# E over two queues, F as fp16 behind the first k loads, and three places of a Linformer-attention and maxout kernel reordered

## The chip, the core and the metric

The kernel runs on one core of a Trainium2 chip. The time is the device time of one execution in microseconds, as the median of several runs. A profile of one execution, with every instruction and DMA packet, goes with it.

## The reference

Attention with keys and values projected along the sequence (Linformer), and behind it a maxout block. All inputs and the output are float32.

```python
k_proj = np.einsum('ks,bhsd->bhkd', E, k)          # E, F: 64 x 1024
v_proj = np.einsum('ks,bhsd->bhkd', F, v)          # q, k, v: 8 batches, 8 heads, 1024, 64
scores = scale * np.matmul(q, k_proj.transpose(0, 1, 3, 2))
attn = np.exp(scores - np.max(scores, axis=-1, keepdims=True))
attn = attn / (np.sum(attn, axis=-1, keepdims=True) + 1e-09)
attn_out = np.matmul(attn, v_proj)
x = attn_out.transpose(0, 2, 1, 3).reshape(B * S, H * D)     # 8192 x 512
h1, h2 = x @ w1, x @ w2                                      # 512 x 1024 each
return np.maximum(h1, h2) @ w_out                            # 1024 x 512
```

## The kernel before

**Algebra.** max(h1, h2) is h2 + relu(h1 - h2). The kernel forms wd = w1 - w2 (`step_wd`, L437) and m = w2 w_out once, and then for each piece of x it computes gt = relu(x wd) (the "up" product) and out = gt w_out + x m (the "down" product). From the second batch on, each of these products of 2x2 blocks is done with seven block products instead of eight, p1 to p7 in the order p1, p2, p6, p5, p7, p3, p4. They need sums of blocks, S(0) to S(3), made by VectorE (`sum_s`, L595), and they share PSUM banks: a bank X takes p1, and p6, p7 and p4 are accumulated onto it in turn; Z takes p5 and then p3; Y takes p2. Each time a bank is to be read before the next product is accumulated, ScalarE copies it to SBUF (`keep`, L607 and L609): s1 after p1, u1 after p6, u2 after p7, s5 after p5. VectorE's `add` (L650 for up, L750 for down) joins two of them into a block.

**Units.** Each of the eight batches has two units, 0 to 15. Unit n's down product is interleaved on TensorE with unit n+1's up product and with the attention of the batches ahead. The interleaving is an order written out by hand: `slots` is a list of keys and functions. ("P", n, p, i) is piece i of down product p of unit n, ("U", n, h, i) the i-th up step of half h, ("G", n, h) a group of attention. `at_slot` hangs further work behind a key. The loop at L906 lays out, for each half h, x pieces, the group, y pieces, and then seven up steps with a piece between each two.

**A group of attention.** `step_group` (L352) issues scores for one group into PSUM banks 2 and 3 (L277) and sums and values for the one before (`step_da`, L380; L289). ScalarE then takes the exponentials of the scores (L370) and the logarithm of the sums (L389). `step_later` runs what `step_da` left for later: at ("U", n, h, 0) the reciprocal by an exponential of minus the logarithm (`invert`, L392), at ("U", n, h, 2) VectorE's multiplication (`finish`, L396).

**Up product p3** of unit n+1 (L673) adds block (0,1), and then, from u2 and s5, block (1,1), each followed by a relu (L653) in the last two units. p4 goes from its bank straight through ScalarE's relu (L690). The sums S(0) and S(1) of the next down product are issued behind them.

**The last unit** has no up product beside its down product (`alone`). There p5 comes before p6 (L812), p5 goes to bank 2, p3 is stored in one piece through ScalarE's queue, and p4 is made in three parts (L792 matmuls, L798 adds) with stores on SyncE's and ScalarE's queues. Its banks are X = 1, Y = 0.

**The start.** SyncE's queue loads E and F as float32 into 64 partitions (L89, L90). GpSimd's queue loads k, q and v of batch 0 in pieces of two heads, cast to fp16 on the way (L101): two k, two q, the identity matrix (made by GpSimd itself, masks.py), two k, two q, four v, then the weights w2 and w1 in pieces (L124, L133). GpSimd's queue holds about eight loads: each further issue waits for the landing of the one eight before. TensorE warms up on a tile of ones (`warm`, L147), transposes E and F in fp32 through the identity (L161), eight transposes each, and VectorE copies the first and ScalarE the second result to one tile `eft` (L168). `step_kv` (L189) multiplies it with k and v, `step_kpt` (L222) and `step_qt` (L248) transpose the projected k and q, `step_sc` makes the scores.

Of the kernel before, what the change touches and what calls it, by code (L numbers as in the profile page):

```python
# [8 lines left out]
FP32 = mybir.dt.float32  # L9
# [7 lines left out]
def kernel(  # L17
# [12 lines left out]
    nc = tc.nc  # L30
# [34 lines left out]
    def att_banks(dtype=FP32):  # L65
# [4 lines left out]
    ctx.enter_context(tc.manual_schedule())  # L70


    nc.scalar.add_instruction(
        mybir.InstLoadActFuncSet(
            name=nc.get_next_instruction_name(),
# [3 lines left out]
            outs=[],  # L79
        )  # L80
    )

    def big(n, dtype=FP16):
        return const.tile([128, 16384 // mybir.dt.size(dtype) // 2], dtype, tag=f"big{n}", name=f"big{n}")

    ef_sb = big(0, FP32)[0:KP, :].rearrange("k (i s) -> k i s", i=2)
    nc.sync.dma_start(out=ef_sb[:, 0, :], in_=E)  # L89
    nc.sync.dma_start(out=ef_sb[:, 1, :], in_=F)  # L90


    def alloc(t, n):
# [14 lines left out]
        alloc(tiles[0], n)  # L108
    for h0 in (0, H // 2):
        for n, src in (("k", k), ("q", q)):  # L110
            for h in (h0, h0 + H // 4):
                load(tiles[0], n, src, 0, h, h + H // 4)
        if h0 == 0:
            ident = const.tile([128, 128], FP32)
            make_identity(nc, ident)
    for h in range(0, H, 2):
        load(tiles[0], "v", v, 0, h, h + 2)

# [34 lines left out]
    nc.vector.tensor_copy(out=ident16, in_=ident)  # L153


    eft = const.tile([128, 2, NC, KP], FP16)
    ef_v = ef_sb.rearrange("kp i (p c) -> kp i c p", c=NC)
    for i in range(2):
        eft_ps = mm_bank()
        for c in range(NC):  # L160
            nc.tensor.transpose(  # L161
                out=eft_ps[:, c * KP : (c + 1) * KP],
                in_=ef_v[:, i, c, :],
                identity=ident[:KP, :KP],
            )
        warm(2)
        eng = nc.scalar.copy if i else nc.vector.tensor_copy
        eng(out=eft[:, i, :, :].rearrange("p c k -> p (c k)"), in_=eft_ps)  # L168

# [7 lines left out]
    def step_kv(t, h0=0, h1=H, which="kv", att=False, dma=False, copy=nc.vector.tensor_copy):  # L179
        kv_ps = att_banks()[:, 0, :] if att else mm_bank()  # L180
        n = (h1 - h0) * D
        both = which == "v"
        nh = 2 if both else h1 - h0
        for h in range(0, h1 - h0, nh):
            for c in range(NC):
                for w in which:
                    i = "kv".index(w)
                    for r in range(2) if both else (i,):
                        nc.tensor.matmul(  # L189
                            out=kv_ps[r * KP : (r + 1) * KP, h * D : (h + nh) * D],  # L190
                            lhsT=eft[:, i, c, :],
                            rhs=t[w][:, h0 + h : h0 + h + nh, c, :],
                            start=(c == 0), stop=(c == NC - 1),
                        )
        fl = lambda ap: ap[:, h0:h1].rearrange("p h z d -> p (h z d)")
        zd = lambda ap: ap.rearrange("p (h d z) -> p h z d", d=D // 2, z=2)
        if "k" in which:
            eng = nc.vector.tensor_copy if which == "k" else nc.scalar.copy
            kp = t["kp"][:, h0:h1]
            k_ps = kv_ps[0:KP, 0:n].rearrange("p (h d) -> p h d", d=D)  # L200
            if dma:
                eng(out=kp, in_=k_ps[:, :, None, :].broadcast_to([KP, h1 - h0, 2, D]))
                step_kpt_dma(t)
            else:
                eng(out=kp[:, :, 0, :], in_=k_ps)
        if both:
            copy(out=t["vp"][:, h0:h1], in_=zd(kv_ps[:, 0:n]))
        elif "v" in which:
            def finish_v():
                nc.vector.tensor_copy(out=t["vp"][KP:128, h0:h1], in_=zd(kv_ps[KP:128, 0:n]))  # L210
                nc.vector.tensor_copy(out=fl(t["vp"][0:KP]), in_=fl(t["vp"][KP:128]))

            if att:
                return finish_v
            finish_v()
# [136 lines left out]
    def step_group(t, g, j, t2, g2, j2):  # L352
        def new():
            if t is None:
                return lambda: None
            banks = [mm_bank(n=2 + e) for e in range(2)]
            score(t, g, j, banks)
            return lambda: scores(t, g, j, banks)

        if t2 is None:  # L360
            new()()
            t_later[0] = None
        else:
            first = (g, j) == (0, 0) and t is not tiles[2]
            acts = None if first else new()
            t_later[0] = step_da(t2, g2, j2, lambda: (new() if first else acts)())

    def scores(t, g, j, banks):
        for e in t["first"]:
# [7 lines left out]
        if t_later[0] is not None:  # L377
            t_later[0] = t_later[0]()

    def step_da(t, g, j, between):  # L380
        if "xt" not in t:
            new_xt(t)
        dn_ps = att_banks()[:, :, 0:W]
        at_ps = att_banks()
        sums_into(t, g, j, dn_ps)
        values_into(t, g, j, [at_ps[:, o, :] for o in range(2)])
        between()
        ld = soft.tile([128, 2, W], FP32, tag="soft", name="ld_sb")
        nc.scalar.activation(out=ld, in_=dn_ps, func=ACTF.Ln)  # L389

        def invert():
            nc.scalar.activation(out=ld, in_=ld, func=ACTF.Exp, scale=-1.0)  # L392
            return finish

        def finish():
            nc.vector.tensor_tensor(  # L396
                out=x_out(t, g, j).rearrange("q z o n -> q o z n"),
                in0=at_ps.rearrange("q o (z n) -> q o z n", z=2),
                in1=ld[:, :, None, :].broadcast_to([128, 2, 2, W]),
                op=ALU.mult,  # L400
            )

        return invert

# [209 lines left out]
    def up_steps(u):  # L616
        for d in range(2):
# [34 lines left out]
            def relu(ap):  # L652
                nc.vector.tensor_scalar_max(ap, ap, 0.0)  # L653
# [17 lines left out]
                st["u2"] = keep("pu", product(7, "X", None))  # L671

            def p3(st=st, product=product, add=add, c_blk=c_blk, d=d):  # L673
                add(0, 1, product(3, "Z", None), st["u1"])
                if u["n"] >= last - 1:
                    relu(c_blk(0, 1))
                    add(1, 1, st["u2"], st["s5"])
                    relu(c_blk(1, 1))
                    return
                add(1, 1, st["u2"], st["s5"])  # L680
                relu(u["gt"][:, NG + 2 * d : NG + 2 * d + 2, :])
# [12 lines left out]
    def down_steps(u, alone):  # L694
# [6 lines left out]

        def product(k, name, n, lo=0, hi=2 * (NG + NX)):
            if n is not None and (lo == 0 or alone):
                st[name] = mm_bank(n=n)
            bank = st[name]
            A = lambda j, h: cat(g_blk(u, j, h), x_blk(u, j, h))
            S = lambda i: cat(s_g(i), s_x(i, u))
# [9 lines left out]
            }[k]()  # L717
            for m in range(lo, hi):
                i, c = divmod(m, NG + NX)
                nc.tensor.matmul(  # L720
                    out=bank[:, i * CH : (i + 1) * CH],
                    lhsT=a(c)[:, i * 128 : (i + 1) * 128],
                    rhs=w_(c),
                    start=(n is not None and m == (lo if alone else 0)),
                    stop=(c == NG + NX - 1), skip_group_check=True,
                )
            return bank
# [17 lines left out]
            else:  # L745
                issue()

        def add(j, c, x, y, queue=nc.sync):
            o_sb = o_tile()
            nc.vector.tensor_tensor(out=o_sb, in0=two(x), in1=two(y), op=ALU.add)  # L750
            store(j, c, o_sb, queue=queue)

        size = 2 * (NG + NX) // (1 if alone else 2 if u["n"] == 0 else 3)

# [13 lines left out]
            st["u1"] = keep("pd", whole(6, "X", None))  # L768

        def p5():  # L770
            st["s5"] = keep("pd", whole(5, "Z", 2 if alone else ybank))

        def p7():
            st["u2"] = keep("pd", whole(7, "X", None))
            if alone:
                add(1, 1, st["u2"], st["s5"])

        def p3():
            add(0, 1, whole(3, "Z", None), st["u1"], nc.scalar if alone else nc.sync)
            if not alone:  # L780
                add(1, 1, st["u2"], st["s5"])

        def p4():
            o_sb = o_tile()
            if alone:
                a = cat(g_blk(u, 1, 1), x_blk(u, 1, 1))
                for i, m0, m1, n, queue in (
                    (0, 0, CH, 3, nc.sync), (1, 0, CH // 2, ybank, nc.scalar), (1, CH // 2, CH, xbank, nc.sync),
                ):
                    bank = mm_bank(n=n)  # L790
                    for c in range(NG + NX):
# [12 lines left out]
            nc.scalar.copy(out=o_sb, in_=two(whole(4, "X", None)))  # L804
            store(1, 0, o_sb)

        steps_ = [
            (p1, 1, "X", xbank), (p2, 2, "Y", ybank), (p6, 6, "X", None), (p5, 5, "Z", ybank),
            (p7, 7, "X", None), (p3, 3, "Z", None), (p4, 4, "X", None),
        ]  # L810
        if alone:
            steps_[2:4] = steps_[3], steps_[2]  # L812
        return [
            (*(lambda a=a, m=m: piece(*a, m) for m in range(0, 2 * (NG + NX) - size, size)), f)
            for f, *a in steps_
# [15 lines left out]
    warm(2)  # L831
    step_kv(t, 4, 8, "k")
    step_dn(t, 0, 0)
    warm(2)
    step_kpt(t, 4, 8)
    step_dn(t, 0, 1)
    step_inv(t, 0, 0)
# [60 lines left out]
    for n, key in enumerate(units):  # L898
# [4 lines left out]
            continue  # L903
        pieces = [(("P", n, p, i), x) for p, x in enumerate(downs) for i, x in enumerate(x)]
        ups = [*up_steps(U[units[n + 1]])]
        for h, (x, y) in enumerate(((6, 1), (1, 1)) if n == 1 else ((2, 2), (2, 3))):  # L906
            slots += pieces[:x]
            slots.append((("G", n, h), lambda: None))
            slots += pieces[x : x + y]
            del pieces[: x + y]  # L910
            for i in range(7):
                slots.append((("U", n, h, i), ups.pop(0)))
                if i < 6:
                    slots.append(pieces.pop(0))
        assert not pieces and not ups

# [69 lines left out]
    for i, (new, old) in enumerate(zip([*groups[1:], none], groups)):  # L986
# [2 lines left out]
            at_slot(("G", n, h), lambda t=new[0], h=h: t.__setitem__("first", (h, 1 - h)))  # L989
        at_slot(("G", n, h), step_group, *new, *old)  # L990
        at_slot(("U", n, h, 0), step_later)
        at_slot(("U", n, h, 2), step_later)

    for n, (b, o) in enumerate(units):
# [58 lines left out]
```

## Time and profile before

| | |
|---|---|
| median of 9 runs | 323.7 us (323.23 to 323.98) |
| profiled execution | 323.98 us |
| its span, first to last instruction | 322.2 us |
| TensorE matmuls busy | 313.9 us, 97% |
| VectorE busy | 236.2 us, 73% |
| ScalarE busy | 209.9 us, 65% |
| granted TensorE clock | 1.00 |

In the profile PE stands for TensorE's matmuls, PEld for its weight loads, DVE for VectorE, ACT for ScalarE, POOL for GpSimd and SP for SyncE. A timeline or chain line begins with its start and its length in us; in brackets stands how long the engine had been idle before it and what ended that. The chain of waits is followed back from the last instruction: it names, for each moment, the engine and line on which the end depended. `xN` is the number of instructions merged into a line. In the DMA view q0 is GpSimd's queue, q1 SyncE's and q10 ScalarE's; a line gives packets, MB and their time as a share of the 16 DMA engines' span.

The span in 40 slices of 8 us, with the busy tenths of PE and of the DMA engines:

```profile
PE   8989999999999999999999999999999999999995
...
DMA  8999999998979999799999999899969131303033
```

PE is busy nearly throughout, except in the first slices and in the last. The DMA engines are full for about the first 230 us, while inputs are loaded.

### The profile page before, as it was taken

The page shows a single profiled execution, that of the slowest core. Times are in us where ns is not written, and L with a number is a line of the kernel's source. Part 1 is how long each engine was busy: PE and PEld are TensorE (multiplying, and loading weights), DVE is VectorE, ACT ScalarE, POOL GpSimd, SP SyncE. Part 2 cuts the span into 40 slices and gives each one's busy share as a digit, 9 for nine tenths or more (in the row PEclk, how much of TensorE's full clock was granted, in tenths as well). Part 3 has the DMA queues.
Part 4 walks back from the last instruction along what each step waited for, and adds up shares of the span by engine and source line. Part 5 has one row for each costly group of instructions (what it writes and reads, how often), then busy time and mean ns, then how long its engine had stood idle before and what let it go on. Part 6 is the DMA issues. An engine that isn't in the chain of part 4 may idle for free.

```text
span 322.2 us, 9141 instructions
## 1 busy us (share of the span) xinstructions
PE 313.9 (97%) x3910; PEld 251.0 (78%) x3910; DVE 236.2 (73%) x419; ACT 209.9 (65%) x373; POOL 43.0 (13%) x67
## 2 busy tenths in 40 slices
PE   8989999999999999999999999999999999999995
PEld 3554587778887888878887888878887888888884
DVE  1365799886967796877967796986967796969672
ACT  2376742767776777667776777767776777765541
POOL 8568102003000400012000300040000000000000
PEclk9999999999999999999999999999999999999999
DMA  8999999998979999799999999899969131303033
GB/s 158 201 200 187 193 207 202 207 186 109 207 146 164 174 213 245 198 191 139 222 226 224 165 210 246 205 150 187 238 140 192 37 100 36 100 33 101 33 132 98
DMA packets 76456, 53.14 MB, mean 165 GB/s; under 512 B 29568, under 2 KB 76288, under 8 KB 76416
## 3 DMA queue, kind: packets, MB, share of 16 engines
q0 software_dynamic: 31008, 28.31, 56.6%
q1 hardware_dynamic: 44992, 23.93, 31.4%
q8 instruction: 30, 0.49, 0.6%
q10 hardware_dynamic: 416, 0.33, 0.3%
q14 instruction: 10, 0.08, 0.1%
HBM read 57.15 MB, written 16.78 MB: 229 GB/s over the span
## 4 chain that ended last, share of the span: by engine, by line
PE 90%; DMA 6%; POOL 2%; issue 1%; DVE 1%; ACT 0%; DVEq 0%; POOLq 0%
PE mm_ps L720 46%; PE mm_ps L635 27%; PE att_ps L189 4%; PE mm_ps L421 3%; PE att_ps L289 3%; DMA big<-in_moe_w_dram 3%; DMA q_sb<-in_q_dram 3%; PE mm_ps L277 2%; PE mm_ps L523 2%; POOL k_sb L101 1%; POOL q_sb L101 1%; PE mm_ps L248 1%; PE mm_ps L792 0%; DVE xt_sb L344 0%; PE mm_ps L446 0%
## 5 line engine op out<-in xcount | busy, mean ns | idle before, releaser
L609 ACT COPY p_sb<-mm_ps 128x512 f32<-128x512 f32 x180 | 101.9, 593 | 45.3 <-PE mm_ps L635 27.7
L720 PEld LDWEIGHTS <-big 128*128 128x128 f16 x768 | 73.5, 98 | 13.1 <-issue 4.4
L720 PE MATMUL mm_ps<-T_sb,big 128*128 128x256 f16 x576 | 78.1, 273 | 0.7 <-ACT p_sb L609 0.7
L650 DVE TENSOR_TENSOR gt_sb<-mm_ps,p_sb 128x512 f16<-128x512 f32 x56 | 38.5, 688 | 45.0 <-PE mm_ps L635 42.1
L635 PE MATMUL mm_ps<-big,big 128*128 128x256 f16 x336 | 50.4, 272 | 0.0
L635 PEld LDWEIGHTS <-big 128*128 128x128 f16 x448 | 43.8, 98 | 5.3 <-issue 0.2
L720 PE MATMUL mm_ps<-wo_sb,gt_sb 128*128 128x256 f16 x256 | 42.8, 273 | 0.0
L720 PEld LDWEIGHTS <-gt_sb 128*128 128x128 f16 x376 | 35.2, 98 | 8.9 <-issue 5.0
L635 PEld LDWEIGHTS <-wd_sb 128*128 128x128 f16 x336 | 32.9, 98 | 3.8
L635 PE MATMUL mm_ps<-xt_sb,wd_sb 128*128 128x256 f16 x224 | 33.6, 273 | 0.0
L370 ACT ACTIVATE ex_sb<-mm_ps 128x512 f16<-128x512 f32 x50 | 27.2, 597 | 8.7 <-PE att_ps L289 7.5
L396 DVE TENSOR_TENSOR xt_sb<-att_ps,ld_sb 128x1024 f16<-128x1024 f32 x26 | 31.7, 1219 | 0.1
L750 DVE TENSOR_TENSOR o_sb<-mm_ps,p_sb 128x512 f32<-128x512 f32 x32 | 21.9, 685 | 6.8 <-PE mm_ps L720 6.7
L240 POOL COPY junk<-qt_sb 1x1 f16<-1x1 f16 x6 | 1.1, 184 | 175.7 <-DMA qt_sb<-q_sb 175.7
L720 PE MATMUL mm_ps<-m_sb,xt_sb 128*128 128x256 f16 x128 | 24.4, 273 | 0.0
L690 ACT ACTIVATE gt_sb<-mm_ps 128x512 f16<-128x512 f32 x28 | 16.8, 600 | 9.5 <-PE mm_ps L635 9.5
L653 DVE TENSOR_SCALAR gt_sb<-gt_sb 128x512 f16<-128x512 f16 (+1 forms) x60 | 21.1, 352 | 2.1
L595 DVE TENSOR_TENSOR big<-gt_sb 128x1024 f16<-128x1024 f16 x32 | 21.9, 685 | 0.2
L720 PE MATMUL mm_ps<-wo_sb,big 128*128 128x256 f16 x128 | 21.5, 273 | 0.0
L720 PE MATMUL mm_ps<-T_sb,gt_sb 128*128 128x256 f16 x120 | 20.3, 273 | 0.0
L720 PEld LDWEIGHTS <-xt_sb 128*128 128x128 f16 x188 | 18.4, 98 | 2.1
L650 DVE TENSOR_TENSOR gt_sb<-p_sb 128x512 f16<-128x512 f32 x28 | 19.1, 682 | 0.0
(102 smaller groups left out, 435.0 us busy)
## 6 DMA issues: line engine op xcount, KB each, us to landing
out_dram<-o_sb SPq DMA_DIRECT2D x62, 256.0 KB, 2.8
k_sb<-in_k_dram POOLq DMA_DIRECT2D x7, 1024.0 KB, 10.3
v_sb<-in_v_dram POOLq DMA_DIRECT2D x7, 1024.0 KB, 16.8
q_sb<-in_q_dram POOLq DMA_DIRECT2D x5, 1024.0 KB, 23.4
q_sb<-in_q_dram POOLq DMA_DIRECT2D x4, 512.0 KB, 18.7
big<-in_moe_w_dram POOLq DMA_DIRECT2D x12, 128.0 KB, 6.9
k_sb<-in_k_dram POOLq DMA_DIRECT2D x4, 256.0 KB, 6.6
q_sb<-in_q_dram POOLq DMA_DIRECT2D x4, 256.0 KB, 7.8
```

The lines of the kernel that those rows point to most:

```text
L189: nc.tensor.matmul(out=kv_ps[r * KP : (r + 1) * KP, h * D : (h + nh) * D], lhsT=eft[:, i, c, :], rhs=t[w][:, h0 + h : h0 + h + nh, c, :], ...
L289: nc.tensor.matmul(out=dst(r ^ (hh % 2))[hh * Z : (hh + 1) * Z, :], lhsT=weights(rows, hh), rhs=ex[rows, hh % 2, hh // 2 * W : (hh // 2 + ...
L370: nc.scalar.activation(out=t["ex", g, j][:, e, :], in_=banks[e], func=ACTF.Exp, scale=scale)
L396: nc.vector.tensor_tensor(out=x_out(t, g, j).rearrange("q z o n -> q o z n"), in0=at_ps.rearrange("q o (z n) -> q o z n", z=2), in1=ld[:, ...
L595: nc.vector.tensor_tensor(out=S(i), in0=S(0) if x is None else x, in1=y(), op=op)
L609: copy(out=x, in_=bank)
L635: nc.tensor.matmul(out=bank[:, m * W : (m + 1) * W], lhsT=w_[:, n_, (2 * d + m) * 128 : (2 * d + m + 1) * 128], rhs=a[:, n_, :], start=(n ...
L650: nc.vector.tensor_tensor(out=c_blk(j, c), in0=two(x), in1=two(y), op=ALU.add)
L653: nc.vector.tensor_scalar_max(ap, ap, 0.0)
L690: nc.scalar.activation(out=out, in_=in_, func=ACTF.Relu)
L720: nc.tensor.matmul(out=bank[:, i * CH : (i + 1) * CH], lhsT=a(c)[:, i * 128 : (i + 1) * 128], rhs=w_(c), start=(n is not None and m == (lo ...
L750: nc.vector.tensor_tensor(out=o_sb, in0=two(x), in1=two(y), op=ALU.add)
```

## The change

- E is loaded in two halves of 512 columns, one below the other into 128 partitions, the first through SyncE's queue and the second through ScalarE's, ahead of the table load. VectorE casts them to fp16 (`e16_sb`).
- F is loaded by GpSimd's queue as fp16 (`f_sb`), behind the four k loads of batch 0 and ahead of its last two q loads. The identity is made behind the first two k loads, ahead of the first q.
- `step_eft(0)` transposes E in fp16, as sixteen 64x64 transposes, and VectorE copies the result from an fp16 bank; `step_eft(1)` does the same for F with eight transposes, and stands where two warm-up matmuls stood, behind the second k product of batch 0. `eft` is two tiles.
- In unit 1 a piece moves from between the last two up steps of half 0 to behind them, and the logarithm of the group ("G", 1, 1) runs at ("U", 1, 1, 0), with the reciprocal at ("U", 1, 1, 1) and the multiplication at ("U", 1, 1, 2) as before.
- In the last unit's up product p3 issues block (1,1) and its relu ahead of block (0,1).
- In the last unit's down product p6 is before p5; p5's two halves go to banks 2 and 3 and are copied by two instructions; block (1,1) is added from p7's bank instead of from its copy; p3 is added and stored by halves over two queues; p4's parts use banks Y, 2 and X.

```diff
+    e_sb = big(0, FP32)[:, 0:HALF]
+    e16_sb, f_sb = (
+        ppool.tile([128, n], FP16, tag="pu", bufs=3, name="ef_sb") for n in (HALF, S)
+    )
+    for r, queue in enumerate((nc.sync, nc.scalar)):
+        queue.dma_start(out=e_sb[r * KP : (r + 1) * KP, :], in_=E[:, r * HALF : (r + 1) * HALF])
...
-    ef_sb = big(0, FP32)[0:KP, :].rearrange("k (i s) -> k i s", i=2)
-    nc.sync.dma_start(out=ef_sb[:, 0, :], in_=E)
-    nc.sync.dma_start(out=ef_sb[:, 1, :], in_=F)
...
         for n, src in (("k", k), ("q", q)):
+            if (h0, n) == (H // 2, "q"):
+                nc.gpsimd.dma_start(out=f_sb[0:KP, :], in_=F)
             for h in (h0, h0 + H // 4):
                 load(tiles[0], n, src, 0, h, h + H // 4)
-        if h0 == 0:
-            ident = const.tile([128, 128], FP32)
-            make_identity(nc, ident)
+            if (h0, n) == (0, "k"):
+                ident = const.tile([128, 128], FP32)
+                make_identity(nc, ident)
...
+    eft = [const.tile([128, NC, KP], FP16, tag=f"eft{i}", name=f"eft{i}") for i in range(2)]
+
+    def step_eft(i):
+        eft_ps = mm_bank(FP16)[:, 0 : NC * KP]
         for c in range(NC):
+            cols = slice(c * KP, (c + 1) * KP)
+            split = lambda w: w.rearrange("q (p c) -> q c p", c=NC)[:, c, :]
+            if i:
+                nc.tensor.transpose(
+                    out=eft_ps[:, cols], in_=split(f_sb[0:KP, :]), identity=ident16[:KP, :KP]
+                )
+                continue
+            for r in range(2):
+                rows = slice(r * KP, (r + 1) * KP)
+                nc.tensor.transpose(
+                    out=eft_ps[rows, cols], in_=split(e16_sb[rows, :]),
+                    identity=ident16[rows, rows],
+                )
         warm(2)
+        nc.vector.tensor_copy(out=eft[i].rearrange("p c k -> p (c k)"), in_=eft_ps)
+
+    nc.vector.tensor_copy(out=e16_sb, in_=e_sb)
+    step_eft(0)
+    warm(2)
...
     step_kv(t, 4, 8, "k")
     step_dn(t, 0, 0)
-    warm(2)
+    step_eft(1)
     step_kpt(t, 4, 8)
...
-        for h, (x, y) in enumerate(((6, 1), (1, 1)) if n == 1 else ((2, 2), (2, 3))):
+        for h, (x, y) in enumerate(((6, 1), (2, 1)) if n == 1 else ((2, 2), (2, 3))):
...
-                if i < 6:
+                if i < 6 - ((n, h) == (1, 0)):
                     slots.append(pieces.pop(0))
...
         at_slot(("U", n, h, 0), step_later)
+        if (n, h) == (1, 1):
+            at_slot(("U", n, h, 1), step_later)
         at_slot(("U", n, h, 2), step_later)
...
-        nc.scalar.activation(out=ld, in_=dn_ps, func=ACTF.Ln)
+
+        def ln():
+            nc.scalar.activation(out=ld, in_=dn_ps, func=ACTF.Ln)
+            return invert
...
-        return invert
+        return ln if ln_later else ln()
```

The last unit, up p3 and then the down product:

```diff
             def p3(st=st, product=product, add=add, c_blk=c_blk, d=d):
-                add(0, 1, product(3, "Z", None), st["u1"])
+                bank = product(3, "Z", None)
+                if u["n"] == last:
+                    add(1, 1, st["u2"], st["s5"])
+                    relu(c_blk(1, 1))
+                add(0, 1, bank, st["u1"])
...
         def p5():
-            st["s5"] = keep("pd", whole(5, "Z", 2 if alone else ybank))
+            if alone:
+                st["s5"] = x = ppool.tile([128, 512], FP32, tag="pd", bufs=4, name="p_sb")
+                for i, bank in enumerate(whole(5, "Z", (2, 3))):
+                    nc.scalar.copy(out=x[:, i * CH : (i + 1) * CH], in_=bank[:, 0:CH])
+                return
+            st["s5"] = keep("pd", whole(5, "Z", ybank))
 
         def p7():
-            st["u2"] = keep("pd", whole(7, "X", None))
+            bank = whole(7, "X", None)
             if alone:
-                add(1, 1, st["u2"], st["s5"])
+                add(1, 1, bank, st["s5"])
+            st["u2"] = keep("pd", bank)
 
         def p3():
-            add(0, 1, whole(3, "Z", None), st["u1"], nc.scalar if alone else nc.sync)
-            if not alone:
-                add(1, 1, st["u2"], st["s5"])
+            if alone:
+                o_sb = o_tile()
+                for i, queue in enumerate((nc.sync, nc.scalar)):
+                    product(3, "Z", None, i * (NG + NX), (i + 1) * (NG + NX))
+                    nc.vector.tensor_tensor(
+                        out=o_sb[:, i, :], in0=st["Z"][i][:, 0:CH],
+                        in1=st["u1"][:, i * CH : (i + 1) * CH], op=ALU.add,
+                    )
+                    store(0, 1, o_sb, i, i + 1, queue=queue)
+                return
...
-                    (0, 0, CH, 3, nc.sync), (1, 0, CH // 2, ybank, nc.scalar), (1, CH // 2, CH, xbank, nc.sync),
+                    (0, 0, CH, ybank, nc.sync), (1, 0, CH // 2, 2, nc.scalar), (1, CH // 2, CH, xbank, nc.sync),
...
-        if alone:
-            steps_[2:4] = steps_[3], steps_[2]
```

## The prediction, as written before the changed kernel was run

> **What bounds the kernel now.** I read the page's busy shares first (PE 313.9 us of a 322.2 us span), then the chain of waits, then timelines of the three places where that chain leaves PE. The span's 322.2 us and about 1.8 us around it make the profiled execution's 323.98 us; the median of the runs is 323.7 us, 0.28 us less, so a sum made on the profile is taken off the median.
>
> The chain of waits, in order of time, in the first 34 us:
>
> ```profile
> 6.89 8.89 DMA q_sb<-in_q_dram
> 15.78 0.29 issue
> 16.07 9.13 DMA big<-in_moe_w_dram
> 25.20 0.03 issue
> ...
> 27.39 0.56 PE att_ps L446 x7
> 27.95 4.32 PE mm_ps L421 x20
> ```
>
> Until 25.2 us the end is set by POOL's queue of loads; from 27.39 us by PE, almost without a gap. The DMA view of two stretches (3.1 to 4.9 us, 7 to 8.8 us) shows what slows that queue at its start:
>
> ```profile
> q1 hardware_dynamic: 86, 0.27, 58.0%
> q0 software_dynamic: 128, 0.13, 49.9%
> ...
> q0 software_dynamic: 368, 0.36, 121.3%
> ```
>
> In 1.8 us POOL's queue (q0) moves 0.36 MB alone, but 0.13 MB while the rest of E and F goes through SP's (q1). It lost 0.23 MB, at 0.2 MB/us some 1.15 us.
>
> PE's chain in unit 1, where two short waits stand in it:
>
> ```profile
> 73.34 0.45 PE mm_ps L635 x4
> 73.79 0.02 issue
> 73.81 0.61 ACT gt_sb L690
> 74.42 0.04 issue
> 74.46 0.41 PE mm_ps L277 x16
> ...
> 77.06 0.44 PE mm_ps L720 x4
> 77.50 0.04 issue
> 77.54 0.60 PE mm_ps L635 x4
> ```
>
> The scores (L277) wait for ACT's relu to free their bank; then L635 waits too. And the last unit, PE's own timeline:
>
> ```profile
> 311.02 2.78 PE L720 MATMUL mm_ps<-T_sb,big 128*128 128x256 f16 x24
> 314.48 1.47 PE L720 MATMUL mm_ps<-T_sb,big 128*128 128x256 f16 x12 [0.67 <-ACT p_sb L609]
> ...
> 318.31 0.28 PE L792 MATMUL mm_ps<-T_sb,xt_sb 128*128 128x128 f16 x2
> ```
>
> The wait named is p7 on the copy of p6's sum out of the same bank. Wherever PE sets the end, a us saved is a us off the time.
>
> **The change, part by part.**
>
> *Start, E and F.* A load's time to landing, added to its issue, gives its arrival. Of batch 0: second k load 8.1 us, second q 10.7, third and fourth k 12.0 and 13.3, third and fourth q 14.6 and 15.8; one about every 1.3 us. PE follows: first k product at 8.25, second at 13.39, the q transposes at 15.63, v at 19.08 after a DMA wait, w at 25.2. So the start is worth what the stream gains. It gains up to 1.15 us at once, since F no longer goes beside the first k. From 2.1 us, where the first packets are, to 3.1 us SP's queue moved 0.52 - 0.27 = 0.25 MB; E alone is 0.26 MB, so E ends about where POOL's packets begin, and I leave 0.15 us for its tail. Then F is paid behind the fourth k. No row shows a 64-row load with a cast. Low end: 64 of the 256 rows of a 1.3 us load, 0.33 us; by the bytes it writes, 0.13 MB at 0.2 MB/us, 0.65 us; high end: as dear as it was, 1.15 us. I take 0.65, as bytes paced every other load of this queue. Net for everything from the third q on: 1.15 - 0.15 - 0.65 = **0.35 us** (0 to 0.8).
>
> The work on E costs nothing if eft is there before the k stream, now at about 7.1 us. E landed 3.6 us after issue (4.34); the halves land no later; a cast (128x512, bounded by 0.34 of a 64x512 fp16 copy and 0.69 of the PSUM cast) ends by 5.0, when PE ends its eight warm-ups (5.06). Sixteen transposes by L222's row (0.31 us for eight) take 0.6, the copy 0.42 (L227, 128x512 fp16): 6.3 us with hand-overs, 0.8 before k. If that cover went, only the first k product would slide, and the fourth q load at 15.4 absorbs up to about 2 us. E's second half on ACT delays the table load by 0.58 us; ACT is first used at 12.41. ident moves before the first q issue: two POOL instructions of 0.25 and 0.29, so both q, two k, F, two q and v issue later; those loads wait 6 to 10 us in the stream anyway. F's issue adds 0.72 there. F's eight transposes (0.5 us by L248) and DVE's copy (0.42) come behind the second k product and replace nothing but the old ACT copy, two warm-ups standing there before and after. From that product to the q transposes PE now needs 2.2 us; 12.4 + 2.2 + 0.5 = 15.1, before 15.4. F itself lands 0.65 after the fourth k, at 13.0, its transposes start at 13.4.
>
> *Unit 1.* A four-matmul piece moves from between the last two up products to behind them. The relu then starts 0.44 us earlier against PE, and PE reaches L277 when it is done: the previous group ends at 74.05, a change to small tiles costs 0.1, so 74.14 instead of 74.46, 0.32 us. The logarithm (0.60) moves behind two copies (1.10 together, from 76.39), which start about 0.5 earlier; the second frees the bank at 77.05 instead of 77.5, and L635 starts at 77.33 instead of 77.54, 0.21 us. What is late next is the logarithm's reciprocal (0.67), to 78.1; DVE's multiplication on it started at 78.45. Sum **0.53 us** (0.2 to 0.53).
>
> *Last unit.* p6 before p5 puts twelve matmuls (1.31 us in the chain) between p6 and p7. The 24 matmuls end at 311.02 + 2.62 = 313.64, p7 began at 314.48: the stall is **0.84 us**, and p6's copy (0.58, from 312.53) now ends 0.5 before p7. In exchange p6 needs S(1) at 310.91, where 312.2 sufficed. S(1) ended at 311.27. The early add(1,1) runs from 307.48 (its copy ends 307.44), before product 3 is there, and closes a gap of DVE from 306.83 to 307.80; S(1) follows 0.5 us earlier, at 310.76. Margin 0.15; I take 0.8 (0.4 if it is half a step late). p5's banks are copied in two parts (0.35 each by L207, for 0.58) under p7; p3's half adds (0.42 each by L798, for 0.69) run under its second half and p4; the add from the bank holds u2's copy until about 316.5, its reader comes at 317.1. Each hidden by a PE step of 1.31.
>
> *Last landing.* The last stores of before stood in one block, each 2.2 to 2.3 us to landing whatever its size, 256 KB or 64 KB. Now the large ones are issued from about 315.9 on and p3's in halves. A store of 256 KB alone landed in 2.1, of which 0.75 is transfer at 350 GB/s; 64 KB alone would be 1.55. So 0 to 0.65 us; with 128 and 64 KB just ahead I take the middle, **0.35**.
>
> The Trainium skill, "DMA: Bandwidth & Descriptors", anatomy of one DMA, speaks against this last term: it puts about 2.0 us of a transfer down as fixed, mostly the target memory's write receipt, and 64 KB would estimate to 2.15 us. By it the last landing gains 0.05, not 0.35, and the whole sum is 1.73, a time of 322.0.
>
> PE's clock: the first eight warm-ups took 0.449 us each, and at 6.01 two took 0.60 together with the drain, so it was full by then. The change takes 2.2 us of fp32 transposes out of 5 to 7.6 us and may leave PE idle for 0.5. "TensorE: Matmul & The Clock Gate" (Part 1) asks for about 3.4 us of busy time in a free-running window; if the gate opened a window late, by that page, matmuls before 9.3 us would run at half speed, some 1 us more, which the fourth q load absorbs: the sum stays.
>
> Sum: 0.35 + 0.53 + 0.8 + 0.35 = 2.03 us; 323.7 - 2.03 = **321.7 us**.
>
> **Rivals.**
> - *The stream is no shorter* (0.17): F costs the 1.0 us it saved. For it: both versions read the same 0.52 MB of E and F on the same engines. Against: F was 4 KB a row in fp32 and is now 2 KB. Gain 1.68, **322.0 us**.
> - *A new wait at the end* (0.15): S(1) misses p6 by half a DVE step, and the last landing stays 2.2 us. For it: the margin of 0.15 and landings alike for all sizes. Gain 0.35 + 0.53 + 0.4 = 1.28, **322.4 us**.
> - *The change doesn't do what it says* (0.07): no shorter stream, one of unit 1's waits comes back (0.2), tail 0.4. Gain 0.6, **323.1 us**, about no change.
> - *Slower* (0.06): F's 64 rows go to two of the 16 DMA engines instead of all. A 1.3 us load is 16 KB an engine, so 64 KB take 5.2 us there, and every later load lands when its slowest engine is done: 5.2 - 1.0 = 4.2 lost, 1.68 gained, **326.2 us**. It decides from three engines down (3.5 - 1.0 = 2.5 lost). Against: E's 0.26 MB, also 64 rows, were through within about a us.
>
> **How the numbers follow.** My forecast has 0.55. Bounds of its terms: best 0.8 + 0.53 + 0.84 + 0.65 = 2.8 (320.9), poorest 0 + 0.2 + 0.4 + 0 = 0.6 (323.1). The range 320.9 to 323.0 leaves out the slower case and part of the third. A difference of 0.2%, 0.65 us, is about what this measurement tells from none: faster is below 323.05. Faster 0.87 (forecast, first two rivals), same 0.07, slower 0.06.
>
> **What would show it.** Right: q0 near 0.36 MB in 1.8 us from 3.3 us on; the first k product at about 7.1 us; the wait for w ending near 24.85; no ACT gt_sb between L635 and the scores at 74 us; p7 following p5 without a gap; the last store under 2 us. Wrong: PE idle on DVE before p6; v and w loads landing later than before; a PE gap on eft near 13 to 15 us.

## The result, and the profile after

Ten runs of the changed kernel have a median of 321.95 us (321.45 to 322.44), thirty of the kernel before 323.7 us (323.05 to 325.7): a ratio of 0.9942, 95% interval 0.993 to 0.9955. Predicted were 321.7 (320.9 to 323.0). Run twice more (e5 and e9 below), the change had 321.85 (0.9928, 0.9903 to 0.9952) and 321.67 (0.9937, 0.992 to 0.9954). The profiled execution of after took 323.26 us, span 321.5: 1.3 us over the median and longer than any of the ten, and where it lost them matters below.

The chain of waits of after, first part (start, duration, what):

```profile
4.74 7.17 DMA k_sb<-in_k_dram
11.90 0.29 issue
12.19 10.50 DMA v_sb<-in_v_dram
22.69 0.29 issue
22.98 5.02 POOL big L135 x7
...
29.92 20.04 DMA v_sb<-in_v_dram
```

Before, loads set the end until 25.2 us. In this execution of after they set it until 49.97: the chain leaves the loads only when batch 1's v has landed. That does not come with every execution: in e9, the same kernel, the chain of waits leaves the loads at 23.13 and follows PE from 23.70 on:

```profile
14.07 9.06 DMA big<-in_moe_w_dram
...
23.70 1.90 PE mm_ps L439 x8
```

The DMA view of after, two stretches (3.3 to 5.1 us, and 7 to 8.8 as before; share of 16 engines last):

```profile
q0 software_dynamic: 310, 0.30, 116.2%
...
q0 software_dynamic: 368, 0.35, 122.5%
```

POOL's queue does start sooner, at 0.30 MB in 1.8 us where 0.36 was forecast and 0.13 stood before (0.13 in 3.1 to 4.9 us; 0.15 in 3.3 to 5.1). PE's timeline of after at the start (start, busy, [idle before it and its releaser]):

```profile
4.98 1.17 PE L172 MATMUL mm_ps<-ident,ef_sb 64*64 64x64 f16 x16
...
8.25 1.03 PE L202 MATMUL mm_ps<-k_sb,eft 128*64 128x256 f16 x8 [1.05 <-DMA k_sb<-in_k_dram]
...
14.58 0.69 PE L166 MATMUL mm_ps<-ident,ef_sb 64*128 64x64 f16 x8
```

PE was ready for k at 7.2 and the first k product still stands at 8.25, where it stood before (8.28). In e5 and e9, the same kernel, it stands at 7.24 and 7.70. Unit 1, the chain of waits of after:

```profile
73.03 0.54 PE mm_ps L745 x4
73.58 0.87 PE mm_ps L653 x8
74.45 0.87 PE mm_ps L745 x8
75.32 0.34 PE mm_ps L290 x16
...
76.53 0.45 PE mm_ps L653 x4
```

L653 was L635, L290 was L277: both waits are gone, and ACT's relu is no longer in the chain. The last unit, PE's timeline of after:

```profile
311.39 0.38 PE L745 MATMUL mm_ps<-m_sb,xt_sb 128*128 128x256 f16 x2
311.61 4.09 PE L745 MATMUL mm_ps<-T_sb,big 128*128 128x256 f16 x36
315.54 0.60 PE L745 MATMUL mm_ps<-wo_sb,big 128*128 128x256 f16 x4
```

Thirty-six matmuls of p6, p5 and p7 in one row, no idle between, where 24 and then a wait of 0.67 stood. DVE's addition for S(1) ends at 311.33, 0.28 before p6 (DVE's timeline of after):

```profile
310.64 0.69 DVE L613 TENSOR_TENSOR big<-big,gt_sb 128x1024 f16<-128x1024 f16 x1
```

And the last stores, DMA issues of after (KB each, us from issue to landing):

```profile
out_dram<-o_sb SPq DMA_DIRECT2D x2, 128.0 KB, 2.0
out_dram<-o_sb ACTq DMA_DIRECT2D x1, 128.0 KB, 2.0
out_dram<-o_sb ACTq DMA_DIRECT2D x1, 64.0 KB, 1.8
out_dram<-o_sb SPq DMA_DIRECT2D x1, 64.0 KB, 1.7
```

The last store of before, in the same view:

```profile
out_dram<-o_sb SPq DMA_DIRECT2D x1, 64.0 KB, 2.2
```

The last 64 KB took 1.7 us for 2.2 before.

### The profile page after: what moved, and what is told of

It is laid out like the page before. It is cut to its first block, busy times and chain, and to the rows that moved or that the text cites. A ratio compares the mean times of both kernels' runs of the same rounds, so it can differ in the third digit from the quotient of the medians.

```text
span 321.5 us, 9162 instructions
## 1 busy us (share of the span) xinstructions
PE 313.5 (98%) x3918; PEld 250.9 (78%) x3918; DVE 237.1 (74%) x422; ACT 209.4 (65%) x373; POOL 44.3 (14%) x68
## 4 chain that ended last, share of the span: by engine, by line
PE 83%; DMA 12%; POOL 3%; issue 1%; DVE 0%; DVEq 0%; POOLq 0%
PE mm_ps L745 46%; PE mm_ps L653 27%; DMA v_sb<-in_v_dram 10%; PE att_ps L202 4%; PE att_ps L302 3%; PE mm_ps L290 2%; DMA k_sb<-in_k_dram 2%; POOL big L135 2%; PE mm_ps L261 1%; POOL k_sb L101 1%; POOL q_sb L101 0%; DVE o_sb L838 0%; POOL wo_sb L139 0%; PE att_ps L290 0%; PE att_ps L235 0%
## 5 line engine op out<-in xcount | busy, mean ns | idle before, releaser
L653 PE MATMUL mm_ps<-big,big 128*128 128x256 f16 x336 | 50.4, 273 | 0.0
L653 PEld LDWEIGHTS <-big 128*128 128x128 f16 x448 | 43.8, 98 | 5.1
L653 PEld LDWEIGHTS <-wd_sb 128*128 128x128 f16 x336 | 32.9, 98 | 3.8
L653 PE MATMUL mm_ps<-xt_sb,wd_sb 128*128 128x256 f16 x224 | 33.6, 273 | 0.0
```

The source lines that it names most:

```text
L653: nc.tensor.matmul(out=bank[:, m * W : (m + 1) * W], lhsT=w_[:, n_, (2 * d + m) * 128 : (2 * d + m + 1) * 128], rhs=a[:, n_, :], start=(n ...
```

## The experiments

The ladder of rungs, us, from one trace of each kernel. Loads: issue plus time to landing. "w": first product with wd (w1 - w2). "u1": first scores of unit 1.

| trace | 2nd k | 4th k | F | 4th q | last v | w | u1 | u1 to PE's end | from there to the span's end |
|---|---|---|---|---|---|---|---|---|---|
| before | 8.15 | 13.29 | | 15.78 | 21.27 | 23.31 | 64.35 | 254.23 | 3.63 |
| e2_unit1 | 8.15 | 13.27 | | 15.77 | 21.50 | 24.17 | 64.62 | 253.70 | 3.65 |
| e3_tail | 8.44 | 13.56 | | 16.07 | 21.32 | 23.47 | 64.04 | 253.39 | 3.14 |
| e4_no_start | 8.30 | 13.44 | | 15.93 | 21.06 | 23.01 | 63.43 | 252.94 | 3.16 |
| e10_no_start | 7.76 | 12.89 | | 15.42 | 21.41 | 23.40 | 64.03 | 252.88 | 3.15 |
| after | 8.11 | 13.23 | 13.86 | 16.39 | 22.69 | 24.57 | 65.46 | 252.87 | 3.15 |
| e1_start | 7.76 | 12.95 | 13.61 | 16.09 | 22.42 | 24.29 | 65.32 | 254.22 | 3.65 |
| e5_after | 7.10 | 12.82 | 13.54 | 15.84 | 21.79 | 23.67 | 64.36 | 252.88 | 3.12 |
| e9_after | 7.56 | 13.07 | 13.51 | 16.05 | 21.81 | 23.70 | 64.26 | 252.87 | 3.15 |
| e6_f_sp | 8.80 | 13.93 | | 16.48 | 21.61 | 25.29 | 65.52 | 252.88 | 3.09 |
| e11_ident_back | 7.29 | 12.70 | 13.46 | 15.65 | 21.24 | 23.98 | 64.35 | 252.88 | 3.14 |
| e12_no_f_in_queue | 7.34 | 12.90 | | 15.41 | 20.78 | 23.08 | 63.29 | 252.96 | 3.15 |
| e7_no_f_load | 7.33 | 12.86 | | 15.46 | 20.84 | 22.88 | 63.54 | 254.22 | 3.70 |
| e8_no_ef_load | 6.33 | 12.65 | | 15.20 | 20.85 | 22.77 | 63.40 | 254.22 | 3.81 |

The last two columns hardly differ between executions of one version, so they measure unit 1 and the end to some 0.1 us. The columns ahead of them differ by up to 1.2 us from execution to execution of the same kernel (u1 of after: 65.46, 64.36, 64.26), so single traces tell little of the start's worth; means and times have to. Most of the 1.3 us that the profiled execution of after took over its median were lost there: its u1 stands 1.1 and 1.2 us behind that of e5 and e9.

One thing holds across all versions. Where the second k lands at 7.76 or later (eight traces), the fourth follows 5.12 to 5.19 us behind it; where it lands at 7.10 to 7.56 (five traces), 5.41 to 5.72 behind; in e8, where it lands at 6.33, 6.32 behind. However early the second k came, the fourth never landed before 12.65.

**e1_start**: the new start alone.

```diff
+    for r, queue in enumerate((nc.sync, nc.scalar)):
+        queue.dma_start(out=e_sb[r * KP : (r + 1) * KP, :], in_=E[:, r * HALF : (r + 1) * HALF])
...
+            if (h0, n) == (H // 2, "q"):
+                nc.gpsimd.dma_start(out=f_sb[0:KP, :], in_=F)
```

> Only the start of the change (E by two queues, F behind the fourth k, identity earlier, transposes in fp16). Theory A, the prediction: the load stream gets 0.35 us shorter from the third q load on, time 0.35 us less than before (0 to 0.8). Theory B, from the profile of the changed kernel, where the loads up to the fourth k land no earlier than before and all behind F about 0.6 us later: the slowest of the DMA engines was never held up by F, so F now costs what it takes there, 0.6 us more than before, and the v transposes of TensorE begin near 18.6 to 19 us instead of 17.98.

Measured 323.88 beside 323.64, ratio 1.0015 (1.0004 to 1.0026). The interval leaves no room for a gain. Theory B's 0.6 more lies inside it (0.1 to 0.8), and the first v product came at 18.73, as B had it.

**e2_unit1**: the piece and the logarithm alone.

```diff
-        for h, (x, y) in enumerate(((6, 1), (1, 1)) if n == 1 else ((2, 2), (2, 3))):
+        for h, (x, y) in enumerate(((6, 1), (2, 1)) if n == 1 else ((2, 2), (2, 3))):
...
-        return invert
+        return ln if ln_later else ln()
```

> Only unit 1's piece and logarithm moved. Theory A: 0.53 us less, no wait of TensorE on ScalarE's relu before the scores near 74 us, none near 77.5 us. Rival: the waits turn up further down (the multiplication that needs the later reciprocal, then the next group's bank), under 0.2 us less.

Measured 323.27, ratio 0.999 (0.998 to 1.0), 0.37 less, which does not decide between 0.53 and the rival's 0.2. The ladder is sharper: u1 to PE's end went from 254.23 to 253.70, 0.53 us.

**e3_tail**: the last unit alone.

```diff
+        if alone:
+            steps_[2:4] = steps_[3], steps_[2]
...
+                for i, queue in enumerate((nc.sync, nc.scalar)):
+                    product(3, "Z", None, i * (NG + NX), (i + 1) * (NG + NX))
```

> Only the last unit. Theory A: TensorE's 36 matmuls of p6, p5 and p7 follow without a gap, 0.8 us less there, and the last store lands 0.35 us sooner after its issue: 1.15 us less in all. Rival, a new wait on VectorE's S(1) and a fixed 2.2 us landing: 0.4 us less.

Measured 322.41, ratio 0.9962 (0.995 to 0.9974), 1.23 less. In the ladder 254.23 - 253.39 = 0.84 for the stall, 3.63 - 3.14 = 0.49 for the last landing.

**e4_no_start**: both of these, the start as before.

```diff
-    for r, queue in enumerate((nc.sync, nc.scalar)):
-        queue.dma_start(out=e_sb[r * KP : (r + 1) * KP, :], in_=E[:, r * HALF : (r + 1) * HALF])
+    nc.sync.dma_start(out=ef_sb[:, 0, :], in_=E)
+    nc.sync.dma_start(out=ef_sb[:, 1, :], in_=F)
```

> The change without its start (E and F as before). Theory A: 1.68 us less than before, so 0.35 us more than the changed kernel. Theory B: 1.85 us less than before or better, so that it beats the changed kernel (1.75 us less) by up to 0.6.

Measured 321.56, ratio 0.9948 (0.993 to 0.9966), a gain of 2.08 where A had 1.68 and B 1.85 or better: without the new start the kernel is as fast as with it.

**e5_after**, **e6_f_sp**, **e7_no_f_load** and **e8_no_ef_load** ran together, beside 324.19 for the kernel before. e5 is the change, unedited.

> The changed kernel once more, beside the others of this set. Theory A (the prediction's start term holds, and the profile of the change was one poor execution): the start gains 0.35, so it is below the kernel without the new start (321.56 beside a before of 323.64, a gain of 2.08): a gain of about 2.4, and in the trace the fourth q load lands before 15.7 us. Theory B (F beside the first k cost the loads little; F in POOL's queue costs all that come behind it 0.63): a gain of 1.5 to 1.9, fourth k landing at 12.9 to 13.3 us, fourth q at 16.1 to 16.4, last v at 22.4 to 22.7.

Measured 321.85, a gain of 2.34, nearer to A. Its rungs are neither's: the fourth k, 12.82, comes just ahead of B's 12.9 to 13.3, the fourth q, 15.84, between A's 15.7 and B's 16.1, and the last v, 21.79, 0.6 earlier than B had it. e6 moves F back to SP's queue:

```diff
+    nc.sync.dma_start(out=f32_sb, in_=F)
...
-            if (h0, n) == (H // 2, "q"):
-                nc.gpsimd.dma_start(out=f_sb[0:KP, :], in_=F)
...
+    nc.scalar.copy(out=f_sb[0:KP, :], in_=f32_sb)
```

> The changed kernel with F's place alone undone: F as fp32 on SP's queue right behind the first half of E, cast by ACT; E by two queues, the fp16 transposes and the rest stay. Theory A: SP's queue takes F's 0.26 MB out of POOL's again, so everything from the third q on lands where it did with F in POOL's queue or later, and the time is that of the change or up to 0.5 us more (321.9 to 322.5). Theory B: the loads behind the fourth k land about 0.6 us earlier than with F in POOL's queue (fourth q at 15.5 to 15.9, last v at about 21.3), and the time is 0.3 to 0.6 us below the change run beside it, near 321.4.

Measured 322.3 (0.9939, 0.9916 to 0.9961), 0.45 above e5 and inside A's 321.9 to 322.5: theory B, that F beside the first k is free, missed. The second k came at 8.80, and PE, which idled for it, paid again. PE's timeline and the windows of e6 (PE busy, PEld, DVE, ACT, POOL, granted clock, DMA share, GB/s):

```profile
8.93 1.89 PE L203 MATMUL mm_ps<-k_sb,eft 128*64 128x256 f16 x8 [1.83 <-DMA k_sb<-in_k_dram]
```

```profile
7.00:9.00 2.00, 0.17 (x2) 0.10 (x2) 0.00 (x0) 1.04 (x1) 1.35 (x2) 0.94 1.21 195
9.00:11.00 2.00, 2.00 (x9) 1.27 (x10) 0.14 (x1) 0.00 (x0) 1.35 (x2) 0.50 1.23 203
```

The first k product took 1.89 us for 1.03, at half the clock, after 1.83 us of idle. The lost clock is not in every execution: two of e6's eight, this one among them, have a mean granted clock of 0.995 and took 323.26 and 323.0 us; the other six, at 0.999 to 1.00, have a median of 322.0, 0.14 above e5. So the 0.45 is F's place and a lost clock together, and B's 0.3 to 0.6 below the change is missed either way. e7 and e8 take the loads away from the kernel before:

```diff
-    nc.sync.dma_start(out=ef_sb[:, 1, :], in_=F)
...
-                in_=ef_v[:, i, c, :],
+                in_=ef_v[:, 0, c, :],
```

> The kernel before without F's load (E's columns stand in for F, so the second projection is computed with E): what F beside the first k costs, by itself. Theory A: POOL's queue gains 1.15 us from the first k on: second k load landing at 7.0, fourth at 12.1, time 322.5. Theory B: landings move by 0.3 at most (second k load 7.8 to 8.2, fourth k 13.0 to 13.3), time 323.3 to 323.7.

Measured 323.32 (0.9978, 0.9962 to 0.9994), 0.87 below its before, between A's 1.2 and B's 0 to 0.4. e8 also leaves out E's load:

```diff
-    nc.sync.dma_start(out=ef_sb[:, 0, :], in_=E)
+    nc.vector.memset(ef_sb[:, 0, :], 0.03)
```

> The kernel before without the loads of E and F (a constant fills E's tile and stands in for both): the floor of the start. Theory A: with 0.52 MB less on the engines the second k load lands at 6.5 to 7.0, the fourth at 11.6 to 12.1, time 322.0 to 322.5. Theory B, in its strict form that POOL's queue paces itself: landings within 0.3 of before (second k 7.8 to 8.2, fourth 13.0 to 13.3), time 323.3 to 323.7. In between (fourth k 12.2 to 12.9): E, not F, is what holds it up.

Measured 323.23 (0.9977, 0.996 to 0.9994). F beside the first k costs some 0.7 us of time (324 x 0.0022, interval 0.2 to 1.2), E nothing that shows. The rungs are neither A's nor B's. The fourth k, 12.65, lies in e8's case in between, but that E is what holds it up is not shown: without F's load alone it landed at 12.86. With nothing to read for E and F, the second k lands 1.82 us earlier than in before, the fourth 0.64, the fourth q 0.58, and w starts 0.54 earlier. What POOL's queue wins at first it gives back. The DMA view of 8 to 10 us, of e8, and of 6 to 8 us, of before:

```profile
DMA packets 325, 0.32 MB, mean 158 GB/s; under 512 B 17, under 2 KB 325, under 8 KB 325
...
DMA packets 399, 0.39 MB, mean 196 GB/s; under 512 B 17, under 2 KB 399, under 8 KB 399
```

In before 0.39 MB went in 6 to 8 and again in 8 to 10 us. And e8's chain of waits at the start has no load in it at all:

```profile
5.06 1.07 PE mm_ps L160 x8
...
6.76 1.02 PE mm_ps L160 x8
...
8.32 0.99 PE mm_ps L188 x8
...
13.45 0.99 PE mm_ps L188 x8
...
17.53 1.94 ACT ex_sb L316 x2
...
22.79 1.88 PE mm_ps L420 x8
```

PE's fp32 transposes (L160), its k products (L188), then ACT's exponentials and PE again: this sequence needs until 22.79 by itself. It is the next limit, 0.5 us under before's 23.31.

**e9_after**, **e10_no_start**, **e11_ident_back** and **e12_no_f_in_queue** ran together, beside 323.87. e9 is the change, e10 is e4 again, each unedited.

> The changed kernel a third time, beside the same without the new start. Theory A (the start gains 0.35): 0.35 us below the kernel without the new start run beside it. Theory C (what E and F take from the loads at the start is given back by 11 us whatever is done there, and F in POOL's queue costs 0.6 to 0.7 behind the fourth k): 0.2 to 0.6 us above it. In the trace, by C: fourth k landing 12.8 to 13.3, F 0.6 to 0.75 behind it, fourth q 15.8 to 16.4.

> Unit 1 and the last unit as changed, the start as before. Theory A: 0.35 us above the changed kernel run beside it (ratio to before near 0.995). Theory C: 0.2 to 0.6 us below it, fourth k landing at 13.2 to 13.6, fourth q at 15.7 to 16.1.

Measured 321.67 (0.992 to 0.9954) and 321.82 (0.9931, 0.9917 to 0.9945). Nothing tells them apart: A's 0.35 is not shown, nor are C's 0.2 to 0.6, of which the sign here is the other. The rungs of e9 lie as C has them (13.07, 16.05), but for F, 0.44 behind the fourth k for 0.6 to 0.75; those of e10 come earlier than C had them (fourth k 12.89 for 13.2 to 13.6, fourth q 15.42 for 15.7 to 16.1). e11:

```diff
-            if (h0, n) == (0, "k"):
-                ident = const.tile([128, 128], FP32)
-                make_identity(nc, ident)
+        if h0 == 0:
+            ident = const.tile([128, 128], FP32)
+            make_identity(nc, ident)
```

> The changed kernel with the identity's two POOL instructions back behind the first two q loads. If they hold up POOL's queue where they stand (the stretch below 180 GB/s right behind them, from 6.0 to 7.0 us in both traces of the change), that stretch moves to 8 to 9.5 us, the second k load lands by up to 0.5 us earlier, and the time stays within 0.2 us of the change, since the fourth k lands the same. If the stretch has another cause, it stays at 6 to 7 us.

Measured 322.23 (0.9949, 0.9933 to 0.9964), 0.56 above e9, more than the 0.2 expected. The second k load lands 0.27 earlier than in e9, but the slow stretch did not move to 8 to 9.5 us: from 5.5 us on, up to 9.5, the only half us of e11 under 180 GB/s is 6.0 to 6.5 (174), and e9 has its own at 7.0 to 8.0 (178 and 170). So the identity's two instructions are not shown to hold up the queue, and what does stays open. The edit shows something else, in PE's timeline of e11:

```profile
5.46 1.17 PE L172 MATMUL mm_ps<-ident,ef_sb 64*64 64x64 f16 x16 [0.40 <-DVE ef_sb L179]
6.56 1.89 PE L149 MATMUL mm_ps<-ones 128*128 128x512 f16 x4
8.38 1.65 PE L202 MATMUL mm_ps<-k_sb,eft 128*64 128x256 f16 x8
```

E's cast now waits for the identity, its transposes start 0.5 later, PE works slowly up to 9.6 us (its clock, see the last section; whether the edit brought that is not shown), and the k product stands at 8.38 although k landed at 7.29. Even at e9's pace, four warm-ups in 1.04 us, it would by estimate have stood at 7.6, so the cover that the prediction named for the work on E (0.8 us) ends here. e12 leaves F's load out of the changed kernel:

```diff
-            if (h0, n) == (H // 2, "q"):
-                nc.gpsimd.dma_start(out=f_sb[0:KP, :], in_=F)
...
+    nc.vector.memset(f_sb[0:KP, :], 0.03)
```

> The changed kernel without F's load (a constant fills F's tile and stands in for it): the price of F in its new place. By the prediction's term F costs 0.65, and by both theories: third and fourth q and all behind land 0.6 to 0.75 us earlier than in the changed kernel beside it, up to the fourth k nothing moves; the time is 0.5 to 0.9 us below the change. Theory A says then that it is 1.0 below the kernel without the new start; theory C that it is within 0.3 us of that kernel. If F in the queue is covered by a later wait, the time moves by less than 0.3.

Measured 321.51 (0.9926, 0.991 to 0.9941): 0.16 below e9, less than 0.5 to 0.9, though the fourth q lands 0.64 earlier and the last v 1.03. The last case of its expectation came: something takes the load's place. The chain of waits of e12:

```profile
13.07 1.00 PE mm_ps L201 x8
...
14.30 0.61 PE mm_ps L164 x8
...
21.58 0.63 ACT ld_sb L341
22.21 0.27 ACT vp_sb L219
22.48 0.04 issue
22.52 0.63 PE att_ps L301 x32
23.15 1.83 PE mm_ps L438 x8
```

F's eight transposes (L164) stand in it, and from the second k product to w no load does. From that product to the first v product PE needs 5.17 us here (13.04 to 18.21) and 4.56 in before (13.42 to 17.98).

## Why the prediction was right, and where it was not

The sum was right, one term was not, and by luck another made up part of it.

**Unit 1, 0.53**: 254.23 - 253.70 = 0.53, and 253.39 - 252.87 = 0.52 between e3 and after, right within the 0.1 us to which this is measured; both waits are gone from the chain.

**Last unit, 0.8 of a stall of 0.84**: 254.23 - 253.39 = 0.84. S(1) came 0.28 us before p6; forecast 0.15. p7 follows without a gap. Both together, 254.23 - 252.87 = 1.36.

**Last landing, 0.35 (0 to 0.65)**: mis-sized; 3.63 - 3.15 = 0.48, of which 0.44 are the last store's landing (2.18 to 1.74 us). By the Trainium skill, "DMA: Bandwidth & Descriptors", anatomy of one DMA, some 2.0 us are fixed and the gain would have been 0.05. The page gives that for GpSimd's path, and these stores go by SyncE's and ScalarE's queues. Here a 64 KB store was down in 1.7 to 1.8 us altogether, so the measurement decides against it in this place.

**Start, 0.35 (0 to 0.8)**: the step that failed. The prediction held that "the start is worth what the stream gains" and that it "gains up to 1.15 us at once". Means over five traces with the old start (before, e2, e3, e4, e10) and four with the new (after, e1, e5, e9):

- second k: 8.16 to 7.63, a gain of 0.53 for 1.0 (1.15 less E's tail); fourth k: 13.29 to 13.02, a gain of 0.27. The gain at first was overrated by half, and it is given back on the way: e8, with neither load, has 1.82 at the second k and 0.64 at the fourth. The 0.36 MB that the gain was read from moved in 7 to 8.8 us; in 3.3 to 5.1 the queue moved 0.27 to 0.32 MB in the four traces with the new start and 0.07 to 0.15 in the five with the old. And a gain of the first 1.8 us was carried on as if nothing else paced the queue.
- F behind it: 0.44 to 0.72, mean 0.61. Forecast 0.65; this price, read from the bytes written, was right.
- Net at the fourth q: 15.79 to 16.09, 0.30 lost, where 0.35 was to be gained.
- Last v: 21.31 to 22.18, 0.87 lost; w 23.47 to 24.06; u1 64.09 to 64.85. Of the last v's 0.87, 0.57 arise behind the fourth q, and why is not settled. They do not come with every execution: the first v lands 2.6 us behind the fourth q in after and e1, but 1.3 in e5 and e9, as in all five with the old start. The mean w of the old start holds e2's 24.17, which is late by PE's clock (see the last section) and not by loads; without it w's loss is 0.76. From batch 1's first projection to u1 there are 15.48 us in e12 and up to 0.61 more in the four traces with the new start (15.61 to 16.09; e3, with the old start, has 15.66), where PE waits for batch 1's v, as in e1:

```profile
49.87 0.38 PE L202 MATMUL att_ps<-v_sb,eft 128*64 128x512 f16 x1 [0.24 <-DMA v_sb<-in_v_dram]
```

In time the loss is smaller than in these traces. Alone the start cost 0.24 (ratio above 1); with the rest, the kernels without it gained 2.08 and 2.05, those with it 1.75, 2.34 and 2.20. The averages, 2.07 and 2.10, are the same. So the start is worth about nothing, within some 0.4 us; a gain of 0.35 is excluded by e1 alone and not shown by any pair. F's load costs 0.7 in its old place (e7) and 0.16 in its new (e12), so A's direction is not absurd; but in the new start the load's removal only uncovers PE's longer sequence, which has F's transposes in it. The prediction hid them behind the fourth q load, with a second k product at 12.4. That product stood at 12.95 to 13.37, and behind it 5.17 us of PE, ACT and DVE follow for 4.56. In after and e1 v's late landing covers that (5.65 and 5.64 us to the first v product); in e5 and e9, as in e12, it is not covered: the first v product comes 5.17 and 5.18 us behind the second k product, 1.0 us after its load has landed. So the step "the start is worth what the stream gains" fails too: PE's own sequence is nearly as long as the stream. Which of the two the chain of waits names differs between executions even of the old start: loads until 22.43 and 22.83 us in e4 and e10, F's load and then PE in e3, PE from its first warm-up on in e2.

The rival "the stream is no shorter" described the start, and gave 322.0. With the measured sizes, 0.53 + 0.84 + 0.48 + 0 = 1.85, or 321.85, beside 321.95, 321.85 and 321.67 measured. The forecast's 2.03 was near by luck: the start's 0.35 too much was half made up by 0.13 more at the landing and 0.04 more at the stall, and the 0.18 left over is within the measurement. The slower rival (F on two DMA engines) is refuted: F took 0.44 to 0.72, not 5.2.

Of what was to show it: the w load that ended the wait at 25.20 before, forecast for 24.85, landed at 25.36, and PE started w at 24.57 for 23.31; "v and w loads landing later than before", listed as a sign against the forecast, is what happened. The 25.20 was late even for the old start: that load landed at 23.78 to 24.66 in the other four, and at 24.48 to 25.36 in the four with the new. The DMA view of 3.3 to 5.1 us was the sign that spoke for it (0.30 MB) and proved nothing for what came 5 us later.

Open: what paces POOL's queue between 6 and 11 us when it has started early, why the last v loses 0.57 more than the fourth q, and whether the start is a few tenths to the good or to the bad. A version that keeps unit 1 and the last unit and leaves the start as it was (e4, e10) is as fast as the change.

## What to carry to other kernels

Read a gain at the head of a queue again at the loads that the critical engine waits for, some loads later: of 1.82 us at the second load 0.64 were left at the fourth. Before a stream is shortened, run the kernel without the load: it shows both the most that can be won (0.54 us at w) and what limits next, here PE's own sequence. Where start times scatter by a us between executions, split the span at a point behind which nothing varies; those parts were measured to 0.1 us, whole times only to 0.5.

## What was not expected of the hardware

- PE's pace at the start differs between executions of the same instructions. In the kernel before two warm-up matmuls at 6.01 us took 0.60 and the first k product 1.03; in e2, with the same start, they took 1.03 and the product 1.77. The view prints a granted clock of 1.00 for both, but the traces hold no record of the clock until full speed begins, at 5.69 us in before, 10.55 in e2 and 9.62 in e11, and there the slow rows end. In e6 the record itself fell to 0.50 at 8.75, 1.65 us into an idle of 1.83, and stayed there for 3.41 us; 1.05 us of idle in after brought no slow row. The Trainium skill, "TensorE: Matmul & The Clock Gate" (Part 1), speaks of about 3.4 us of idle before the clock falls, in a window that runs freely; here, in the one trace where it fell, less than 2 us were enough.
- Sixteen fp16 transposes of 64x64 took 1.17 us at 4.98, where eight at 9.79 took 0.31: nearly twice the 0.6 that was worked out from the later row. F's eight took 0.69 at 14.58, for a forecast of 0.5. The clock is not the reason: in e9, at full speed from 5.23 on, the sixteen took 1.14.
- A load on POOL's queue of 64 rows, 0.13 MB written, landed 0.44 to 0.76 us behind the load ahead of it (five traces), some half of a 0.26 MB load's 1.3.
